# DeltaNet attention with a folded feed-forward on one core: odd heads on the other partition half, weight signs on GpSimd, second inverse in PSUM, a new order of work

## The chip, the core and the metric

The kernel runs on one core of one Trainium2 chip. The metric is the time of one execution on the device in microseconds (us). The kernel before takes 628.66 us, the median of 3 runs (627.59 to 628.71). A profile is one more execution, recorded by the hardware profiler. Its *span* is a little shorter than the time, because the time also holds the start and the end: the profiled execution of before had a span of 623.6 us and a time of 625.4 us. The runs of a program on one core can fall into a slower state.

Engine names in the profile: PE is the matrix engine, PEld its weight loads (they overlap PE), DVE the vector engine, ACT the scalar engine, POOL is GpSimd, SP the engine that issues most DMA transfers. L474 is line 474 of the kernel that was profiled, so the same statement has different numbers in different kernels.

## The reference

The attention is a delta rule with one 48 x 48 state for each of 4 batches and 8 heads, over 768 steps. The feed-forward part takes its result as 3072 tokens of 384 features.

```python
# q, k, v: (B=4, H=8, S=768, D=48), beta: (B, H, S)
k_n = k / (norm(k) + 1e-6)
for t in range(S):
    y[:, :, t] = q[:, :, t] @ state
    v_old = state^T k_n[:, :, t]
    state = state + beta_t * outer(k_n[:, :, t], v[:, :, t] - v_old)
x = y as (B*S, H*D)                    # 3072 x 384
a, b = x @ w1, x @ w2                  # 384 x 1024 each
out = ((a * b) @ w3) @ w_out           # 1024 x 1024, 1024 x 384; weights come as float64
```

## The kernel before

The sequence is cut into 12 chunks of 64 tokens. Inside a chunk the delta rule becomes the inverse of a triangular 64 x 64 matrix for each head and batch, some products with it, and an update of the state. Two chunks make a pair, and each pair feeds 512 tokens to the feed-forward part. There the product w3 @ w_out is formed once (`fold`), so that only three large products remain per token: with w1, with w2 and with the folded weight.

The program is a set of generators (`scores`, `inverse`, `chain`, `ab`, `piece` and so on). A long string, ORDER, names the generator that takes its next step. Every engine executes its instructions in exactly that order. Its letters: `P` weight pieces, `V` inverses, `c` chain, `s` scores, `g` and `N` sums of squares and norms, `a` and `o` feed-forward products, `f` folding.

The weights arrive as float64 and are converted with integer arithmetic, in 36 pieces. For each piece ACT scales twice, DVE shifts and puts the sign in, and GpSimd adds the low bits exactly:

```python
def piece(n, srcs, dst):
    raw = in_turn(ffn, [P, CW, 2], "raw", 5, "raw", U32)      # five raw buffers
    ...                                                       # DMA on the SP queue
    act.activation(out=dst, in_=hi.bitcast(FP32), func=ACTF.Abs, scale=2.0**-112)
    act.activation(out=lo, in_=lo, func=ACTF.Copy, scale=2.0**-29)
    yield
    dve.tensor_scalar(out=du, in0=du, scalar1=3, scalar2=None, op0=ALU.logical_shift_left)
    dve.scalar_tensor_tensor(
        out=du, in0=hi, scalar=0x80000000, in1=du, op0=ALU.bitwise_and, op1=ALU.bitwise_or
    )
    yield
    pool.tensor_tensor(out=du, in0=du, in1=lo, op=ALU.add)
```

The inverse of a pair is 31 steps of two DVE operations. Its working matrix V is in SBUF, except for the first pair, where it is held in PSUM:

```python
    V = Vb                                  # SBUF
    if j == 0:
        V = two_banks().rearrange("p a (s t) -> p (a s) t", t=BS)    # PSUM
        ...
    for s in range(BS - 1):
        ...                                 # tb = V * U
        dve.tensor_tensor(out=o, in0=o, in1=tv, op=ALU.subtract)
        yield
```

The small products of the chain are 64 x 64 or 48 x 64 tiles. I call the half of the 128 partitions on which a product's inputs lie its row half, the half on which its output lies its column half, and the pair of the two a *quarter*; there are four. In `by_tokens`, which makes X, both halves are `half(z)`, so that only the two diagonal quarters are used:

```python
    def by_tokens(ps, r, h, z):
        return ps[half(z), r, D * h : D * h + D]
    ...
    ps = products(
        by_tokens, lambda r, h, z: TT[half(z), r, h, :], lambda r, h, z: R[half(z), r, h, :]
    )
```

## Time and profile before

| | before |
|---|---|
| time, median of 3 | 628.66 us |
| span of the profiled execution | 623.6 us |
| first feed-forward matmul with w1 starts | 139.44 us |
| PE busy after that | 479.2 of 480.4 us |
| PE busy before that | 101.1 of 139.4 us, clock 0.85 |
| first feed-forward product taken by DVE | 155.98 us |

I call what lies before 139.4 us the *front* and what follows the *dense part*. The prediction below shows the lines and reads them in this order.

One more view divides the front of before into three legs along DVE's work: first inverse, from the first to the second inverse, second inverse. The columns are start and end, length, then busy time and instructions of PE, PEld, DVE, ACT and POOL, the granted PE clock, the DMA share and GB/s.

```profile
44.13:74.30 30.17, 23.88 (x74) 14.68 (x73) 27.86 (x78) 11.98 (x25) 12.77 (x12) 0.84 0.85 192
74.30:123.39 49.09, 44.89 (x917) 32.01 (x918) 40.69 (x68) 26.41 (x51) 23.03 (x22) 0.86 0.77 176
123.39:155.90 32.51, 28.21 (x145) 14.44 (x134) 30.41 (x71) 11.41 (x25) 6.50 (x5) 0.95 0.76 128
```

The third column of busy times is DVE: 27.9 of 30.2 us, 40.7 of 49.1, 30.4 of 32.5. DVE is the busiest engine in the first and the last leg. A blocked DVE instruction counts as busy here.

### The profile page before, as it was taken

To read this page: it belongs to the slowest core of one execution; us is meant where nothing else is said; L and a number is where in the kernel's file an instruction comes from. 1 tells how busy PE (TensorE), PEld (TensorE's weight loads), DVE (VectorE), ACT (ScalarE), POOL (GpSimd) and SP (SyncE) were. 2 spreads that over 40 slices of the span, in tenths; PEclk is the share of its full clock that TensorE was granted. 3 is DMA by queue.
4 is the path that set the end of the run, shared out by engine and by line. 5 is a ranking of instruction groups with operands and counts; after the bars stand their busy time and mean duration, and the time that the engine had idled before them with its cause. 6 is when DMAs were issued, how large, how long until landed. Compare 5 with 4: busy or idle time off the path is not lost.

```text
span 623.6 us, 17022 instructions
## 1 busy us (share of the span) xinstructions
PE 580.3 (93%) x7372; PEld 343.1 (55%) x7372; DVE 352.2 (56%) x764; ACT 161.1 (26%) x333; POOL 102.1 (16%) x114
## 2 busy tenths in 40 slices
PE   3838779979999999999999999999999999999997
PEld 2724457744575655665556655466564556545454
DVE  3599879999856674667827659464397032100100
ACT  3573236642241112311113111123011022210100
POOL 5364453402321100201002010120001000000000
PEclk9857888999999999999999999999999999999999
DMA  9678966886742724443444453333311200000001
GB/s 207 163 211 169 239 153 140 195 150 107 174 65 52 126 76 87 64 77 80 70 106 52 68 120 73 68 67 43 69 40 39 72 23 3 26 14 25 0 14 38
DMA packets 201835, 55.60 MB, mean 89 GB/s; under 512 B 191969, under 2 KB 195041, under 8 KB 201761
## 3 DMA queue, kind: packets, MB, share of 16 engines
q1 hardware_dynamic: 197600, 53.74, 41.7%
q10 hardware_dynamic: 4160, 0.79, 0.8%
q8 instruction: 58, 0.95, 0.7%
q14 instruction: 17, 0.13, 0.1%
HBM read 42.30 MB, written 11.01 MB: 85 GB/s over the span
## 4 chain that ended last, share of the span: by engine, by line
PE 81%; DMA 7%; SPq 4%; DVE 3%; issue 2%; ACT 2%; POOL 1%; DVEq 0%; ACTq 0%; POOLq 0%
PE ps_f L694 41%; PE ps_f L714 20%; PE ps_w L474 6%; PE ps_w L569 4%; PE ps_w L322 3%; DMA raw<-in_moe_w_dram 3%; SPq L212 2%; PE ps_t L444 2%; PE ps_t L430 2%; PE ps_f L674 2%; DMA vtok<-in_v_dram 1%; DMA ktok<-in_k_dram 1%; DMA X<-in_q_dram 1%; DMA raw<-in_moe_w_out_dram 1%; SPq L614 1%
## 5 line engine op out<-in xcount | busy, mean ns | idle before, releaser
L694 PE MATMUL ps_f<-xT,w1s 128*128 128x512 f32 x288 | 132.9, 605 | 4.3 <-DMA xT<-xT 4.3
L694 PE MATMUL ps_f<-xT,w2s 128*128 128x512 f32 x288 | 131.7, 599 | 0.0
L714 PE MATMUL ps_f<-w,ab 128*128 128x384 f32 x384 | 126.4, 488 | 0.0
L714 PEld LDWEIGHTS ps_f<-w,ab 128*128 128x128 f32 x384 | 72.5, 190 | 51.1 <-issue 3.0
L708 DVE TENSOR_TENSOR ab<-a,ps_f 128x512 f32<-128x512 f32 x48 | 32.5, 683 | 112.7 <-PE ps_f L694 112.6
L694 PEld LDWEIGHTS ps_f<-xT,w1s 128*128 128x128 f32 x288 | 53.9, 192 | 66.0 <-issue 63.2
L694 PEld LDWEIGHTS ps_f<-xT,w2s 128*128 128x128 f32 x288 | 53.1, 190 | 60.3 <-issue 56.8
L703 ACT COPY a<-ps_f 128x512 f32<-128x512 f32 x48 | 27.5, 586 | 142.6 <-PE ps_f L694 132.9
L391 DVE TENSOR_TENSOR tb<-Vb,Ub 128x31 f32<-128x31 f32 (+15 forms) x155 | 55.5, 358 | 13.0 <-DMA Ub<-Ud 8.2
L396 DVE TENSOR_TENSOR Vb<-Vb,tb 128x31 f32<-128x31 f32 (+15 forms) x155 | 58.4, 377 | 5.3
L674 PE MATMUL ps_f<-w2s,w3T 128*128 128x384 f32 x128 | 50.0, 550 | 3.6 <-POOL w2s L630 2.1
L234 POOL TENSOR_TENSOR sq<-ktok 128x384 f32<-128x384 f32 x24 | 20.7, 862 | 152.0 <-DVE ss L236 91.6
L590 ACT COPY xT<-ps_w 48x256 f32<-48x256 f32 x96 | 30.4, 365 | 54.2 <-PE ps_w L569 53.7
L720 ACT COPY osb<-ps_f 128x384 f32<-128x384 f32 x24 | 11.3, 479 | 127.4 <-PE ps_f L714 109.1
L460 POOL TENSOR_TENSOR vtok<-vtok,n 128x384 f32<-128x384 f32 x24 | 19.9, 842 | 130.6 <-DMA vtok<-in_v_dram 104.3
L674 PEld LDWEIGHTS ps_f<-w2s,w3T 128*128 128x128 f32 x128 | 26.8, 215 | 23.3 <-issue 6.9
L322 PE MATMUL ps_w<-KQ 48*64 48x128 f32 x768 | 30.5, 303 | 5.3 <-DVE KQ L285 2.7
L322 PEld LDWEIGHTS ps_w<-KQ 48*64 48x64 f32 x768 | 25.0, 150 | 13.9 <-issue 5.5
L665 PE MATMUL ps_f<-ident,w 128*128 128x128 f32 x64 | 13.4, 363 | 13.5 <-POOL w L630 13.5
L630 POOL TENSOR_TENSOR w<-w,raw 128x512 uint32<-128x512 uint32 x16 | 21.2, 1332 | 26.6 <-ACT w L622 7.8
L534 DVE TENSOR_TENSOR S<-S,ps_w 48x768 f32<-48x768 f32 x20 | 19.0, 949 | 11.0 <-PE ps_w L474 10.7
L331 DVE TENSOR_TENSOR U<-ps_w,wt 128x512 f32<-128x512 f32 x24 | 16.4, 686 | 15.0 <-PE ps_w L322 14.6
(83 smaller groups left out, 558.3 us busy)
## 6 DMA issues: line engine op xcount, KB each, us to landing
raw<-in_moe_w_dram SPq DMA_DIRECT2D x16, 512.0 KB, 6.2
vtok<-in_v_dram SPq DMA_DIRECT2D x24, 192.0 KB, 4.0
raw<-in_moe_w_dram SPq DMA_DIRECT2D x24, 192.0 KB, 4.0
out_dram<-osb SPq DMA_DIRECT2D x24, 192.0 KB, 2.0
ktok<-in_k_dram SPq DMA_DIRECT2D x22, 192.0 KB, 4.3
raw<-in_moe_w_out_dram SPq DMA_DIRECT2D x8, 384.0 KB, 3.8
Ud<-U SPq DMA_DIRECT2D x48, 64.0 KB, 2.0
Ub<-Ud SPq DMA_DIRECT2D x6, 512.0 KB, 4.6
```

Of the source, the lines that this page charges most:

```text
L322: pe.matmul(ps[half(z), h % 2, 128 * (h // 2) : 128 * (h // 2) + 128], lhsT=x[:, 0, :], rhs=x.rearrange("p j t -> p (j t)"), start=True, s ...
L391: dve.tensor_tensor(out=tv, in0=V[:, 0 : s + 1, s : s + 1].to_broadcast([P, s + 1, n]), in1=U[:, s, s + 1 : BS].unsqueeze(1).to_broadcast( ...
L396: dve.tensor_tensor(out=o, in0=o, in1=tv, op=ALU.subtract)
L474: pe.matmul(out(ps, r, h, z), lhsT=lhs(r, h, z), rhs=rhs(r, h, z), start=True, stop=True,)
L569: i = pe.matmul(region(h, z, r), lhsT=lhs, rhs=rhs, start=part[n] not in part[:n], stop=part[n] not in part[n + 1 :],)
L590: act.copy(out=xT[f, p:NP:2, b : b + NR, cc, :].rearrange("p a r t -> p r a t"), in_=pyv[f, z, b : b + NR],)
L630: pool.tensor_tensor(out=du, in0=du, in1=lo, op=ALU.add)
L674: pe.matmul(ps[:, 0:DM], lhsT=w3Ts[jc, kc // 4][:, kc % 4 * P : kc % 4 * P + P], rhs=wo[:, kc], start=(kc == 0), stop=(kc == KF - 1),)
L694: pe.matmul(ps[:], lhsT=w[:, m, js], rhs=x[:, m].rearrange("p b c t -> p (b c t)"), start=(m == 0), stop=(m == KM - 1),)
L703: act.copy(out=a[:], in_=ps[:])
L708: dve.tensor_tensor(out=t[:], in0=a[:], in1=ps[:], op=ALU.mult)
L714: pe.matmul(ps[:, 0:DM], lhsT=abs_[u, jc][:, b * P : (b + 1) * P], rhs=w34[:, jc, :], start=(jc == 0), stop=(jc == KF - 1),)
```

## The change

It is four things in one diff.

1. *Crossing.* The keys, the masked scores and X of the odd heads move to the other partition half. The product that makes X and the product that uses it then rotate over all four quarters of the array. It costs twice the DMA issues for k (four of 96 KB for a chunk instead of two of 192 KB), scores of odd heads as two matmuls of 64 columns instead of one of 128, and an exchange (`across`) of the norms' sums and of the weights between the halves, twice for each pair.
2. *Signs.* DVE's sign operation goes. ACT takes the sign of the high word, GpSimd multiplies by it.
3. *Second inverse in PSUM* (`if j < 2`).
4. *A new ORDER*, different from the first step to the last, made for the new operations.

```diff
 ORDER = """
-P3 P6 k0 g0 q0 P3 P3 P3 g0 g0 k1 K0 K0 P6 P6 K0 K0 K0 Q0 Q0 Q0 Q0 Q0 g0 g0 g0 g0 K1 K1 K1 K1
+P6 k0 q0 K0 g0 k1 beta K0 K0 K0 P0 P6 K0 g0 P11 g0 Q0 g0 Q0 g0 g0 g0 P6 P6 g0 q1 Q0 Q0 Q0 P0
 ... (all other lines of the string differ too)
+    def across(src, dst):
+        ...
+        for z in range(2):
+            pe.matmul(
+                psv[half(1 - z)], lhsT=ident[half(z), half(z)], rhs=odd[half(z), 1],
+                start=True, stop=True,
+            )
+        yield
+        dve.tensor_copy(out=even[:, 0], in_=odd[:, 0])
+        dve.tensor_copy(out=even[:, 1], in_=psv)
 ... scores:
-                    pe.matmul(
-                        ps[half(z), h % 2, 128 * (h // 2) : 128 * (h // 2) + 128],
-                        lhsT=x[:, 0, :], rhs=x.rearrange("p j t -> p (j t)"),
+                    if h % 2 == 0:
+                        (as before)
+                    else:
+                        for j in range(2):
+                            pe.matmul(
+                                ps[half(z ^ j), 1, n + C * j : n + C * j + C],
+                                lhsT=x[:, 0, :], rhs=x[:, j, :], start=True, stop=True,
+                            )
 ... inverse:
-        if j == 0:
+        if j < 2:
 ... chain:
-        def by_tokens(ps, r, h, z):
-            return ps[half(z), r, D * h : D * h + D]
+        def crossed(ps, r, h, z):
+            g = NP * r + h // 2
+            return ps[half((z + h) % 2), h % 2, D * g : D * g + D]
 ... outputs:
-                        todo.append((h, z, r, X[half(z), r, h, :], PT[half(z), r, h, :]))
+                            x = half((z + h) % 2)
+                            todo.append((h, z, r, X[x, r, h, :], PT[x, r, h, :]))
 ... piece:
+        act.activation(out=hi.bitcast(FP32), in_=hi.bitcast(FP32), func=ACTF.Sign)
         yield
         dve.tensor_scalar(out=du, in0=du, scalar1=3, scalar2=None, op0=ALU.logical_shift_left)
-        dve.scalar_tensor_tensor(
-            out=du, in0=hi, scalar=0x80000000, in1=du, op0=ALU.bitwise_and, op1=ALU.bitwise_or
-        )
         yield
         pool.tensor_tensor(out=du, in0=du, in1=lo, op=ALU.add)
+        pool.tensor_tensor(out=dst, in0=dst, in1=hi.bitcast(FP32), op=ALU.mult)
```

## The prediction

> **What bounds the kernel now.** I began with the busy shares and slices of the page, cut the span where the first feed-forward matmul starts, and asked for the busy times of both stretches.
>
> ```profile
> PE   3838779979999999999999999999999999999997
> DVE  3599879999856674667827659464397032100100
> POOL 5364453402321100201002010120001000000000
> PEclk9857888999999999999999999999999999999999
> 0.00:139.40 139.40, 101.11 (x1484) 71.37 (x1484) 109.12 (x227) 68.61 (x132) 60.99 (x65) 0.85 0.82 181
> 139.40:619.80 480.40, 479.18 (x5888) 271.72 (x5888) 243.06 (x538) 92.02 (x202) 41.07 (x49) 1.00 0.32 62
> ```
>
> The last two rows give length, then busy PE, weight loads, DVE, ACT, POOL, the granted clock, DMA share and GB/s. There are two kernels here. After 139.4 us PE is busy for 479.2 of 480.4 us at full clock: whatever shortens a PE instruction shortens the run, and other engines cost nothing unless they starve PE. Before it, PE is busy for 101 of 139 us at clock 0.85. DVE is busy for 109 and DMA for 82%; there a chain through DVE, the DMA queue and PE decides when the dense part begins. So time = start of the dense part + its PE work + about 4 us of last store.
>
> What releases the dense part I read from the timeline and the chain of waits:
>
> ```profile
> 139.44 1.19 PE L694 MATMUL ps_f<-xT,w1s 128*128 128x512 f32 x1 [4.30 <-DMA xT<-xT]
> 155.98 0.68 DVE L708 TENSOR_TENSOR ab<-a,ps_f 128x512 f32<-128x512 f32 x1
> ```
>
> PE waited only 4.3 us for xT, but DVE could first take a feed-forward product at 155.98, right after the second inverse (123.39 to 155.9) ended in its order. Three result banks and four a-halves bridge those 16.5 us and hardly more. The end of the second inverse is therefore the second gate, and an earlier xT alone would gain little.
>
> Why DVE is slow there is visible when GpSimd works beside it:
>
> ```profile
> 63.33 1.28 POOL L630 TENSOR_TENSOR w<-w,raw 128x512 uint32<-128x512 uint32 x1 [1.27 <-DVE w L626]
> 63.44 0.43 DVE L396 TENSOR_TENSOR ps_w<-ps_w,tb 128x255 f32<-128x255 f32 x1
> ...
> 127.20 1.28 POOL L630 TENSOR_TENSOR w1s<-w1s,raw 128x512 uint32<-128x512 uint32 x1 [2.55 <-DVE w1s L626]
> 127.29 1.33 DVE L396 TENSOR_TENSOR Vb<-Vb,tb 128x112 f32<-128x112 f32 x1
> ```
>
> In PSUM (first inverse) 255 columns take 0.43 us beside GpSimd; in SBUF (second inverse) 112 columns take 1.33 us, until GpSimd is done. Undisturbed they take 0.28.
>
> **The Trainium skill.** (1) "SBUF — State Buffer", section "SBUF: two separate sides": DVE and GpSimd share one port pair as an exclusive lock, taken by a DVE instruction with two SBUF inputs or in a 2-port mode. The four lines agree. (2) "VectorE: DVE Perf Modes", "The perf-mode tier table": fp32 tensor_scalar from SBUF runs 2x, tensor_tensor 1x. The trace agrees (TENSOR_SCALAR of 512 columns undisturbed 0.42 us, the two-input sign operation 0.69), so the remaining TENSOR_SCALAR can be blocked by GpSimd too; one took 1.32. (3) "TensorE: Matmul & The Clock Gate", "LDWEIGHTS": columns / 1.2 ns, so 64 columns are 53 ns. Next paragraph. (4) Same page, Part 3: tiles of different position run together.
>
> **Part 1, inverse products on four quarters.** Same 64 weight columns, same 48 moving columns:
>
> ```profile
> L474 PE MATMUL ps_w<-R,TT 64*64 64x48 f32 x704 | 22.7, 219 | 0.0
> L474 PE MATMUL ps_w<-S,KQ 48*64 48x48 f32 x704 | 12.6, 220 | 0.0
> L322 PE MATMUL ps_w<-KQ 48*64 48x128 f32 x768 | 30.5, 303 | 5.3 <-DVE KQ L285 2.7 <-ACT KQ L307 2.4 <-ACT xT L590 0.2
> ```
>
> R,TT sits on the two diagonal quarters and costs 22.7/704 = 32.2 ns each; S,KQ uses all four and costs 12.6/704 = 17.9. Two of 32.2 are 64 ns, four of 17.9 are 72: both near the load of one quarter (53 ns by the skill, plus gaps), so each quarter is limited by its weights and two more quarters nearly double the rate. The change makes R,TT (with the first chunk's vtok,TT) rotate over four quarters. I count 640 of the 768 instructions after the first feed-forward matmul: 640 x 14.3 ns = -9.2 us; 128 in the front, where PE has slack.
>
> **Part 2, scores.** Odd heads split a 128-column matmul into two of 64, because the masked part must land on the other half: per chunk 96 PE instructions instead of 64. Moving columns are unchanged; only loads are added. A warm chunk takes 1.91 us (chain of waits), 16 rounds of about 119 ns on four quarters. An odd quarter now needs two rounds like S,KQ, 2 x 58 to 67 ns = 117 to 134. I take +7%, 0.13 us a chunk, 8 chunks in the dense part: +1.0 us. If the new order hinders overlap it could be +30%, +4.6 us.
>
> **Part 3, crossing of norms and weights.** Twelve times two tiny matmuls through a feed-forward bank and two DVE copies. PE pays mainly the switch: a lone block of six feed-forward matmuls takes 2.77 us against 2.58 inside a run, 0.19; with the matmuls I put 0.25 each, eight in the dense part: +2.0. DVE: 24 copies, by the 0.2 us of its small operations 5 us in all, hidden.
>
> Dense part: -9.2 + 1.0 + 2.0 = -6.2 us.
>
> **Part 4, signs on GpSimd.** Removed from DVE: 36 sign operations, 15.5 + 11.1 + 5.6 = 32.2 us, nearly all in the front. Added to ACT: 36 Sign, like the 36 scalings there (23.2 us): 68.6 + 23 is harmless in some 120. Added to GpSimd: 36 multiplies like its adds, 21.2 + 15.7 + 8.3 = 45.2 us, about 30 of them (38 us) before the dense part: 61 + 38 = 99 of 120 us. That is close.
>
> **Part 5, second inverse in PSUM; new order.** I summed undisturbed durations in DVE's order. To the end of the second inverse: 117 us before (actual 155.9, the rest is waiting), 96 after. By legs: the first inverse, 44.13 to 74.3, starts about 2 us earlier (no blocked sign operations ahead; its data could come at 39.5) and loses 4.3 us of signs, of which about 1.3 comes back in blocked TENSOR_SCALARs: -5. From there to the second inverse DVE falls from 36 to 27 us of work. The DMA queue between the store of the first inverse (75.4) and the load of the second's U (118.8) goes from 52 issues in 43.4 us to 43; in proportion -7.5. DVE and queue agree: -8. The second inverse, 32.5 us, loses 2.8 us of signs and some 3 of blocking, takes 1.7 us more TENSOR_SCALAR work: -4. Sum -17. GpSimd at above 80% will block TENSOR_SCALARs and hold raw buffers longer, so the queue stalls: +4. Front: -13; dense part from about 126.
>
> DMA allows it: the front moved 181 GB/s x 139.4 us = 25 MB. The new order issues two fewer w1/w2 pieces (1 MB) and one chunk fewer of small kperm transfers before xT, and can raise its 82% share a little. It would not allow -25.
>
> Total: 628.7 - 13 - 6.2 = 609.5, say 609 us.
>
> **Rivals.** (a) GpSimd becomes the bound in the front: its last adds and the raw buffers hold back weights and with them the folding on PE. For: 99 of 120 us and slow two-input work (1.33 us per 512 columns). Against: the piece rate is also set by DMA (512 KB, 6.2 us to landing), and GpSimd is idle in long stretches now. Front gain 3: 619. (b) The dense part starves: it comes earlier, while DVE still owes the third inverse and GpSimd weight pieces; the inverse held in PSUM leaves one two-bank buffer for chain and scores. For: DVE's sevens to nines up to slice 30. Against: DVE loses work overall and the first inverse already lived so. Some +5: 614. (c) Scores and crossings cost more than I put, up to +8 on PE, eating part 1: 615. (d) The front follows DVE's relief of 21 us fully: 601. (e) Nothing gained in front, part 1 cancelled: 628, needs (a) and (c) together.
>
> **Range and chances.** The front is the wide term, -3 to -21; the dense part -9 to 0. Together 80% within 598 to 621. Two per cent is 616.1: I give 0.76 to faster, 0.22 to same, 0.02 to slower.
>
> **What would show it.** R,TT near 18 ns each, 13.7 us in all; scores at 2.0 to 2.1 us a warm chunk; crossings at 0.25; first w1s matmul at 120 to 130, second inverse ending about 15 us later without 1.3 us steps; PE in the stretch after it above 99% busy and 474 us long. Wrong if the first w1s matmul comes after 135 with GpSimd busy before it, or if idle PE appears behind it, or if the scores' instructions rise above 2.5 us a chunk.

## The result, and the profile after

The changed kernel takes 611.0 us, the median of 4 runs (610.54 to 613.09), against 628.22 us for the kernel before in 4 runs (627.59 to 628.71). The ratio is 0.9733 with a 95% interval from 0.9707 to 0.9759: faster. The output is correct. A ratio in this document is the mean time of one kernel's fast runs over that of the other's of the same rounds, so it is not quite the ratio of the medians that are quoted.

The profiled spans are 623.6 and 608.8 us, a difference of 14.8 us. The medians differ by 17.2 us, because the profiled run of before was a quick one (625.4 us against its median of 628.2). What follows explains the 14.8.

These are the slices of the page of after, in tenths of busy time.

```profile
PE   3728998989999999999999999999999999999997
DVE  2659975578745954766964539675384231101100
POOL 5778866576340010200031001310000000000000
PEclk9856997999999999999999999999999999999999
```

In the first ten slices GpSimd's row now has fives to eights, where before it had nothing above six and mostly three to five. PE's row has eights and nines from the fourth slice on. The same execution in two stretches, cut where its first w1 matmul starts:

```profile
0.00:130.70 130.70, 98.17 (x1629) 69.27 (x1629) 88.06 (x206) 84.55 (x161) 92.69 (x93) 0.86 0.79 182
130.70:605.00 474.30, 470.67 (x6176) 263.99 (x6176) 235.70 (x547) 98.33 (x211) 52.31 (x58) 1.00 0.34 67
```

The front is 130.7 instead of 139.4 us long, so 8.7 us came from there. In it DVE fell from 109.1 to 88.1 us of work, and GpSimd rose from 61.0 to 92.7. The dense part is 474.3 instead of 480.4 us long, so it gave 6.1 us. PE's work there fell by 8.5 us (479.18 to 470.67), but its gaps grew from 1.2 to 3.6 us.

The two gates in the timeline of after, the first w1 matmul and the first product that DVE could take, are these:

```profile
130.69 1.53 PE L742 MATMUL ps_f<-xT,w1s 128*128 128x512 f32 x3 [1.60 <-DMA xT<-xT]
...
147.32 0.68 DVE L756 TENSOR_TENSOR ab<-a,ps_f 128x512 f32<-128x512 f32 x1
```

Both moved by the same 8.7 us (139.44 to 130.69, 155.98 to 147.32). The distance between them is 16.5 and 16.6 us. The end of the second inverse is again the second gate; here DVE does two more operations between (and waits 0.67 us for keys), so the product comes 1.6 us after it instead of 0.1.

In the groups of after, the columns are engine, operation, output and inputs, shapes and count, then busy time in us and the mean in ns of one. A mean is from start to modelled end, and such small matmuls overlap: the rate is busy time over count.

```profile
L517 PE MATMUL ps_w<-R,TT 64*64 64x48 f32 x704 | 12.9, 220 | 0.1
L618 PE MATMUL ps_w<-PT,X 64*48 64x64 f32 x768 | 12.9, 216 | 0.0
L251 PE MATMUL ps_f<-wt,ident 64*64 64x16 f32 x24 | 1.8, 220 | 0.0
L251 PE MATMUL ps_f<-ss,ident 64*64 64x16 f32 x24 | 1.8, 219 | 0.7 <-ACT w L729 0.6
```

R,TT took 22.7 us and takes 12.9, which is 12.9 / 704 = 18.3 ns each against 32.2. The product of masked scores and X also became cheaper. In the groups of before it read:

```profile
L569 PE MATMUL ps_w<-PT,X 64*48 64x64 f32 x768 | 16.1, 219 | 0.1
```

That is 3.2 us less for the whole run, which I had not predicted. Its even heads and its odd heads used to run in two separate modes; now all rotate over four quarters in one. The versions below show that both savings are the crossing's: R,TT takes 22.7 to 23.1 us and masked scores by X 16.1 to 16.4 us in every kernel without it, 12.6 to 14.5 and 12.9 to 13.5 in every one with it, whatever the order. That a quarter is limited by its weights, as the prediction says, and not by something else that the quarters do not share, no run tests.

The same three legs of the front in after:

```profile
41.85:70.86 29.01, 23.18 (x68) 13.54 (x69) 27.15 (x70) 19.36 (x36) 24.94 (x22) 0.75 0.85 224
70.86:110.92 40.06, 36.45 (x784) 26.46 (x783) 27.49 (x54) 26.59 (x51) 27.00 (x24) 0.91 0.72 157
110.92:145.72 34.80, 32.72 (x337) 17.94 (x336) 25.45 (x74) 20.96 (x41) 24.10 (x21) 1.00 0.79 168
```

The first leg starts 2.3 us earlier and is 1.2 us shorter. The middle leg is 9.0 us shorter. The third leg has 5.0 us less of DVE work (30.41 to 25.45) and yet is 2.3 us longer: DVE's idle time in it rose from 2.1 to 9.35 us. What it waits for stands in the timeline of after:

```profile
115.02 0.67 ACT L671 ACTIVATE w1s<-raw 128x512 f32<-128x512 f32 x1 [1.80 <-DMA raw<-in_moe_w_dram]
115.72 0.43 DVE L675 TENSOR_SCALAR w1s<-w1s 128x512 uint32<-128x512 uint32 x1 [3.54 <-ACT w1s L671]
...
135.53 0.68 ACT L671 ACTIVATE w2s<-raw 128x512 f32<-128x512 f32 x1 [5.44 <-DMA raw<-in_moe_w_dram]
136.24 0.43 DVE L675 TENSOR_SCALAR w2s<-w2s 128x512 uint32<-128x512 uint32 x1 [2.69 <-ACT w2s L671]
```

The order places the shifts of weight pieces between steps of the inverse. Here the inverse stands still because a piece is not there: DVE waits for ACT, and ACT waits for the DMA of the raw weights. Four such gaps (3.54, 2.69, 0.88 and 0.41) make 7.5 us. The queue shows why. These are the issues of weight pieces on the SP queue during the second inverse of before (start, how long the issues took, and their number; a piece of w1 or w2 is four issues):

```profile
125.96 3.67 SPq L614 DMA_DIRECT2D raw<-in_moe_w_dram  x8
...
131.09 3.56 SPq L614 DMA_DIRECT2D raw<-in_moe_w_dram  x4
...
145.85 1.72 SPq L614 DMA_DIRECT2D raw<-in_moe_w_dram  x4
```

And of after:

```profile
107.88 8.35 SPq L663 DMA_DIRECT2D raw<-in_moe_w_dram  x12
...
117.76 5.29 SPq L663 DMA_DIRECT2D raw<-in_moe_w_dram  x8
...
130.56 1.92 SPq L663 DMA_DIRECT2D raw<-in_moe_w_dram  x4
...
135.39 4.20 SPq L663 DMA_DIRECT2D raw<-in_moe_w_dram  x8
```

The new order brings eight pieces (32 issues) through the queue in this leg, the old one four (16 issues). From 107.4 to 145.7 us the queue of after is issuing for 37.4 of 38.3 us. It is full, and the inverse waits for what stands in it. How much of a piece's lateness is its issue and how much its transfer is not separated here: the DMA engines were busy for 79% of this leg, in before for 76%.

### The profile page after: what moved, and what is told of

Read it like the earlier page. It is cut to its first block, busy times and chain, and to the rows that moved or that the text cites.

```text
span 608.8 us, 17988 instructions
## 1 busy us (share of the span) xinstructions
PE 569.2 (94%) x7804; PEld 333.2 (55%) x7804; DVE 323.8 (53%) x752; ACT 183.4 (30%) x373; POOL 145.0 (24%) x150
## 4 chain that ended last, share of the span: by engine, by line
PE 71%; DMA 8%; SPq 8%; DVE 6%; POOL 2%; issue 2%; ACT 1%; POOLq 0%; DVEq 0%; ACTq 0%
PE ps_f L742 36%; PE ps_f L762 21%; SPq L226 4%; PE ps_w L517 4%; PE ps_w L618 3%; DMA raw<-in_moe_w_dram 2%; PE ps_t L487 2%; SPq L663 2%; PE ps_w L366 2%; PE ps_t L473 1%; PE ps_w L360 1%; DVE ps_w L439 1%; DVE tb L434 1%; DMA Ub<-Ud 1%; DVE w L675 1%
## 5 line engine op out<-in xcount | busy, mean ns | idle before, releaser
L742 PE MATMUL ps_f<-xT,w1s 128*128 128x512 f32 x288 | 131.1, 598 | 1.6 <-DMA xT<-xT 1.6
L762 PE MATMUL ps_f<-w,ab 128*128 128x384 f32 x384 | 127.3, 488 | 0.0
L266 POOL TENSOR_TENSOR sq<-ktok 128x384 f32<-128x384 f32 x24 | 20.6, 858 | 156.5 <-DVE ss L268 98.9
L434 DVE TENSOR_TENSOR tb<-Vb,Ub 128x31 f32<-128x31 f32 (+15 forms) x124 | 43.5, 351 | 7.1 <-DMA Ub<-Ud 3.1
L439 DVE TENSOR_TENSOR Vb<-Vb,tb 128x31 f32<-128x31 f32 (+15 forms) x124 | 43.0, 347 | 4.3
L768 ACT COPY osb<-ps_f 128x384 f32<-128x384 f32 x24 | 11.4, 479 | 109.6 <-PE ps_f L762 81.5
L360 PEld LDWEIGHTS ps_w<-KQ 48*64 48x64 f32 x384 | 25.8, 152 | 9.7 <-ACT KQ L343 4.0
L366 PE MATMUL ps_w<-KQ 48*64 48x64 f32 x768 | 30.9, 241 | 0.0
L581 DVE TENSOR_TENSOR S<-S,ps_w 48x768 f32<-48x768 f32 x20 | 19.0, 949 | 19.3 <-PE ps_w L517 14.4
L366 PEld LDWEIGHTS ps_w<-KQ 48*64 48x64 f32 x768 | 28.5, 153 | 0.1
L713 PE MATMUL ps_f<-ident,w 128*128 128x128 f32 x64 | 11.4, 320 | 14.4 <-POOL w L678 12.1
```

The source lines that it names most:

```text
L360: pe.matmul(ps[half(z), 0, n : n + 128], lhsT=x[:, 0, :], rhs=x.rearrange("p j t -> p (j t)"), start=True, stop=True,)
L366: pe.matmul(ps[half(z ^ j), 1, n + C * j : n + C * j + C], lhsT=x[:, 0, :], rhs=x[:, j, :], start=True, stop=True,)
L434: dve.tensor_tensor(out=tv, in0=V[:, 0 : s + 1, s : s + 1].to_broadcast([P, s + 1, n]), in1=U[:, s, s + 1 : BS].unsqueeze(1).to_broadcast( ...
L742: pe.matmul(ps[:], lhsT=w[:, m, js], rhs=x[:, m].rearrange("p b c t -> p (b c t)"), start=(m == 0), stop=(m == KM - 1),)
L762: pe.matmul(ps[:, 0:DM], lhsT=abs_[u, jc][:, b * P : (b + 1) * P], rhs=w34[:, jc, :], start=(jc == 0), stop=(jc == KF - 1),)
```

## The experiments

The prediction added up parts. So the first theory was: **the parts act separately**, each is worth what its own operations save, and the order only has to fit. The first rival was that **the new order itself** brings the front's gain, whatever the operations. The second was that **the parts are worth something only in an order made for them**. A further rival, (a) of the prediction, was that **GpSimd bounds the front** now. Twelve kernels were run, in three jobs on the chip, all with a correct result. One timed run of b_all and three of a_nocross were slow; medians and ratios leave them out. Medians of before in the three jobs: 628.61, 628.15 and 628.0 us. The changed kernel was not run again in these jobs; "slower than after" compares with its 611.0 us, which holds to about the 0.6 us by which the medians of before differ. "Before" and "after" name the operations and the order that a version starts from.

| version | order | operations | median us | minus before of its job | ratio, 95% interval |
|---|---|---|---|---|---|
| b_sign | old | before + signs | 638.66 | +10.0 | 1.0153 (1.0116 to 1.0191) |
| b_v1 | old | before + PSUM inverse | 627.69 | -0.9 | 0.9990 (0.9956 to 1.0023) |
| b_cross | old | before + crossing | 665.78 | +37.2 | 1.0606 (1.0569 to 1.0642) |
| b_all | old | all of after | 672.37 | +43.8 | 1.0700 (1.0638 to 1.0762) |
| b_order | new | before | 642.75 | +14.6 | 1.0222 (1.0174 to 1.0270) |
| a_nosign | new | after, signs undone | 616.08 | -12.1 | 0.9798 (0.9754 to 0.9841) |
| a_nov1 | new | after, PSUM inverse undone | 623.14 | -5.0 | 0.9911 (0.9884 to 0.9938) |
| a_nocross | new | after, crossing undone | 632.06 | +3.9 | 1.0039 (1.0014 to 1.0065) |
| b_cross2 | old, exchanges later | before + crossing | 651.9 | +23.9 | 1.0390 (1.0353 to 1.0428) |
| a_exch | new, exchanges earlier | after | 624.98 | -3.0 | 0.9949 (0.9931 to 0.9967) |
| a_actq | new | after, 16 loads on ACT's queue | 624.98 | -3.0 | 0.9958 (0.9937 to 0.9979) |
| a_half | new | after, 8 of 36 signs back | 612.65 | -15.4 | 0.9763 (0.9722 to 0.9804) |

### b_sign: the signs alone, in the old order

```diff
+        act.activation(out=hi.bitcast(FP32), in_=hi.bitcast(FP32), func=ACTF.Sign)
-        dve.scalar_tensor_tensor(out=du, in0=hi, scalar=0x80000000, in1=du, ...)
+        pool.tensor_tensor(out=dst, in0=dst, in1=hi.bitcast(FP32), op=ALU.mult)
```

> The kernel before, its own order, with the signs alone moved from DVE to ACT and GpSimd. Theory (the front is a chain in which DVE, the DMA queue and the order share): DVE loses some 28 us of busy time, but the queue's order is as before, so the first w1s matmul moves from 139.4 to about 135 and the time falls by 4 us (1 to 8). Rival 1 (the signs alone make the front's gain): first w1s at about 130, -9 us. Rival 2 (GpSimd becomes the bound without the new order): no gain or slower, with GpSimd above 85% busy before the first w1s matmul.

It is 10 us slower instead of faster. The dense part begins at 148.93 us, 9.5 us later than in before, so the loss is in the front. The longest wait of PE in b_sign (total, times, longest) is:

```profile
PE ps_f L662 <- POOL w L627: 25.6, 6, 8.5
```

In before the same wait, of the transposes of w3 for GpSimd's result, was 13.5 us. Here GpSimd is busy for 94.9 us of the front, about as in after (92.7). That is 64% of the longer front, not the 85% that rival 2 named. What differs is when the result is asked for: the old order places the transposes for the old GpSimd work, and each piece now takes GpSimd twice as long. This is read from the waits (after, with the same work in its own order, waits for 12.1 us there); no run moved the transposes alone.

### b_v1: the second inverse in PSUM alone, in the old order

```diff
-        if j == 0:
+        if j < 2:
 (twice; and four more V1 steps in the order, for the copies into and out of PSUM)
```

> The kernel before, its own order, with the second inverse alone in PSUM. Theory: the blocked steps of the second inverse (some five of over 1 us) vanish, it ends 3 to 4 us earlier less 1.2 us of copies; xT comes as before, so the time falls by 0 to 3 us. Rival (the held two-bank buffer starves chain and scores): slower by 2 us or more, with PE waiting for ps_w.

The time did not move clear of noise (ratio 0.999, interval across 1), which lies in the range. The inverse did get shorter, from 32.5 to about 29 us, but it started 4 us later (127.3 instead of 123.4), and the dense part began at 144.43. The first product that DVE took came at 157.58, against 155.98. The later start need not be the edit's: DVE was 3.5 us behind before's trace at 101 us already, ahead of every step of the second inverse, and the profiled run was the slowest of the four (629.08). The old order has few GpSimd operations beside this inverse (6.5 us of POOL in before's third leg), so there was less blocking to escape than in the new one.

### b_cross and b_all: the crossing alone, and all three parts, in the old order

The first builds of this version deadlocked and were not run: with a fixed order, an exchange can wait for a bank that only a later step frees. So in b_cross the exchange uses the bank of `corner`, and one step of `corner` moved up a little in three of the six pairs:

```diff
-        ps = bank([P, n, NR, NP])
+        ps = in_turn(psT, [P, n, NR, NP], "t", 1, "ps_t")
 (otherwise the code of after, with `if j == 0` and the sign operation of before;
  the 24 steps of the exchanges stand directly behind the sums and the norms)
```

> The kernel before, its order, with the crossing alone (crossed loads, scores, products, outputs and the 12 exchanges, which here take the corner's PSUM bank instead of a feed-forward bank so that the old order stays free of deadlock). Theory: the dense part is 6 us shorter, the front unchanged: -6 us (4 to 9), R,TT at 18 ns each. Rival (exchanges and scores eat it when the order was not made for them): within 2 us of before.

b_all is the code of after in the old order, with the same bank for the exchange and the same placing.

> All three parts of the change in the old order (exchanges in the corner's PSUM bank). Theory: -6 from the crossing and about -5 from the front, -11 us, so the new order is worth some 6 us by itself on top. Rival (the new order is worth nothing by itself): -17 us, as the change.

Both missed by far: +37 us and +44 us. PE's longest waits in b_cross:

```profile
PE ps_t L249 <- DVE wt L297: 18.0, 5, 4.2
PE ps_f L712 <- POOL w L677: 16.2, 4, 5.4
```

The exchange is a matmul whose input is the end of a chain of 15 small DVE operations. Standing directly behind it in the order, it makes PE wait for that chain, 18.0 / 5 = 3.6 us on average. The work itself was predicted at 0.25 us, and measured in after at (1.8 + 1.8) / 12 = 0.3. Here the price of an exchange is the wait, not the work. The waits are not the only loss. The dense part of b_cross begins at 154.3 and is 506.7 us long with PE busy for 486.65, at a clock of 0.96; after needs 470.67 us for as many instructions at a clock of 1.00. So the 8.5 us that the crossing saves on PE in after do not appear here. Why the clock is lower was not tested.

The parts add up among themselves: +10.0 - 0.9 + 37.2 = +46.3 against +43.8 for all three together, whose fast runs lie between 668 and 676 us. So the sum shows no interaction beyond the noise. The order is what turns a loss of 44 us into a gain of 17. (b_all differs from after in the exchange's bank too, so this compares the order with that bank. And "the old order" includes my placing of the exchanges: b_cross2 below takes 13.9 us of the loss away by another one.)

### b_order: the new order with the operations of before

The code of before, with the string of after less the 28 steps that only the new operations have.

> The new order alone, with the kernel before's operations. Theory: the order was made for a relieved DVE; alone it gives the queue's part of the front, -3 us (-7 to +3) against before. Rival (the order makes the front's gain): -9 us or more.

It is 14.6 us slower, where I expected a gain of 3. The first rival falls: the order has no gain of its own. Its stretches:

```profile
134.40:637.10 502.70, 485.00 (x5889) 273.19 (x5887) 250.52 (x551) 94.69 (x204) 44.27 (x51) 0.99 0.32 63
```

The dense part starts 5 us earlier than in before, but it holds 17.7 us of idle PE. The second inverse runs from 115.83 to 159.65, 43.8 us, and DVE takes the first product only at 161.47, 27 us after the dense part began. The distance that is bridged without loss was 16.5 us. About half of the idle time, 9.0 us, falls between 142 and 164 us, around this late product; most of the rest, 7.7 us, comes later, has no releaser in the profile and is looked at under a_nocross.

### a_nosign: after, with the signs back on DVE

The three edits of b_sign, reversed, in the code of after.

> The changed kernel with its order, the signs put back on DVE alone. Theory: DVE regains 30 us before the dense part, first w1s matmul from 130.7 to about 137, time some 6 us above the changed kernel (617). Rival (the front's gain is the new order of the DMA queue): within 2 us of the changed kernel (611).

It came as expected, 5 us slower than after. The first w1 matmul is at 135.07 and the first product at 153.56. DVE is busy for 101.5 us of that front, against 88.1 in after. In the new order the signs are worth 5 us on GpSimd; in the old one they cost 10.

The second inverse of this version is telling. It has the same weight pieces beside it, and DVE does their signs as well; yet it takes 35.4 us (115.52 to 150.97), only 0.6 more than in after. DVE's waits for pieces in it are 1.83 and 0.18 us instead of 7.5:

```profile
119.34 0.43 DVE L672 TENSOR_SCALAR w1s<-w1s 128x512 uint32<-128x512 uint32 x1 [1.83 <-ACT w1s L669]
...
140.76 0.43 DVE L672 TENSOR_SCALAR w2s<-w2s 128x512 uint32<-128x512 uint32 x1 [0.18 <-ACT w2s L669]
```

So in this leg the relief from the signs seems to have been spent almost wholly on waiting for the same pieces.

### a_nov1: after, with the second inverse back in SBUF

```diff
-        if j < 2:
+        if j == 0:
 (twice; four V1 steps out)
```

> The changed kernel with its order, the second inverse back in SBUF alone. Theory: GpSimd is 70% busy beside it, so many of the 62 steps wait for it (up to 1 us each); the inverse takes some 6 to 10 us more and the dense part starves by about as much: 616 to 620 us. Rival (the inverse was not on the path): 611.

It is 12 us slower than after, more than I expected. The second inverse takes 44.9 us (114.11 to 159.01) instead of 34.8. One pair of steps shows it. In a_nov1, with V in SBUF:

```profile
134.28 1.39 DVE L437 TENSOR_TENSOR Vb<-Vb,tb 128x255 f32<-128x255 f32 x1
```

In after, with V in PSUM, at the same shape:

```profile
128.02 0.43 DVE L439 TENSOR_TENSOR ps_w<-ps_w,tb 128x255 f32<-128x255 f32 x1
```

GpSimd works beside this inverse in both, for 24.8 us in a_nov1 and 24.1 in after. DVE's busy time in it, which holds the time in which an instruction is blocked, is 40.8 us in a_nov1 and 25.5 in after. The new order puts many weight pieces beside this inverse. That is worth it only with the inverse in PSUM; b_order shows what the same order does without.

### a_nocross: after, without the crossing

The keys, scores, X and outputs as before; the 24 steps of the exchanges taken out of the new order.

> The changed kernel's order with signs on GpSimd and the second inverse in PSUM, but without the crossing. Theory: the dense part is 6 us longer, plus 1 us: about 617 to 618. Rival (the crossing's worth is hidden in the order): 611.

It is 21 us slower than after, where I expected 6 to 7. The front is as good as in after (first w1 matmul 129.78, first product 147.04). Its dense part:

```profile
129.80:622.70 492.90, 479.79 (x5889) 271.42 (x5888) 235.76 (x534) 99.29 (x214) 53.37 (x59) 1.00 0.33 64
```

PE is busy for 9.1 us more than in after (479.79 against 470.67), which is the crossing's own worth on PE: it agrees with the 8.5 us between before and after. The other 9.5 us are idle time (13.1 against 3.6). Most of that idle time, 8.4 us in six stretches, the profile lays to no releaser. The 20 runs spread from 625.0 to 636.3 us, and the profile fell in one of the quicker ones (628.21), so the two halves explain its span and not the whole 21 us.

The trace has more to say of the 8.4 us. b_order, which shares the order and lacks the crossing too, has six such stretches at nearly the same places of PE's stream, 7.7 us; before and after have none of over 0.5 us. The pages list a queue q8 "instruction" that moves 16 KB at a time: 58 transfers in kernels with 7372 matmul records and as many weight loads, 61 in those with 7804. All six stretches of a_nocross end 1.3 to 1.5 us after such a transfer has ended, as do those of b_order. In all twelve versions together there are 35 of over 0.5 us, and each ends 1.3 to 1.8 us after one. So PE most likely waited for its own next instructions. Why they come late with this order and without the crossing was not tested.

This version also answers another question. It loads k in two transfers per chunk, as before does, and yet DVE waits for the same two weight pieces inside the second inverse for 3.14 and 2.88 us. So the extra k issues of the crossing are not what makes the pieces late.

### b_cross2: the old order with the exchanges later

If the wait for the weights' exchange is what makes b_cross slow, it should shrink when the exchange stands just before the product that needs it.

```diff
-N0 N0 N0 P15 s0 s0 s0 q1 ... s1 f0 e1 c0
+N0 P15 s0 s0 s0 q1 ... s1 f0 e1 N0 N0 c0
 (likewise for the other five pairs)
```

> As the crossing alone in the old order, but the six exchanges of the weights stand later in PE's order, just ahead of the product whose result they scale, instead of directly behind the norms. Theory (PE executes in order and stood still for 18.0 us before these exchanges while DVE worked out the norms): the time falls from 665.8 by about 20 us, to 640 to 650, and the wait for DVE wt is gone from PE's list. Rival (the crossed loads or the scores cost it): it stays above 660.

The wait of 18.0 us is gone, and the time fell by 13.9 us, from 665.78 to 651.9, just short of the expected 640 to 650. That settles the largest single part. The remaining 24 us above before have many small parts. In the profiled run the front is 10.6 us longer than in before (150.0), and PE is idle for 17.4 us in the dense part instead of 1.2. The largest wait of PE that is left is

```profile
PE ps_f L712 <- POOL w L677: 15.7, 4, 4.9
```

It is near the 13.5 us of before. What causes the rest was not resolved.

### a_exch: after, with the exchanges earlier

The same test from the other side. The second half of `norms` is moved directly behind the first in the new order (for the third pair nine steps behind).

```diff
-... beta P7 N0 P7 P7 s0 s0 s0 ... t3 N0 P4 P1 P13 P2 P2 V0 t3 P10 P10 t2 P13 N0
+... beta P7 N0 N0 N0 P7 P7 s0 s0 s0 ... t3 P4 P1 P13 P2 P2 V0 t3 P10 P10 t2 P13
```

> The changed kernel with one thing of its order undone: the exchanges of the weights stand directly behind the norms in program order. Theory: PE waits some 3 to 4 us at each of five exchanges in the dense part and front, +10 to +18 us: 621 to 629. Rival (with this order DVE is done early and the place does not matter): within 3 us of 611.

It is 14 us slower than after, within the range, and the wait is back:

```profile
PE ps_f L249 <- DVE wt L297: 14.7, 5, 5.7
```

No operation was added or removed here. Twelve steps in another place cost 14 of the 17 us that the change brings.

### a_actq: after, with 16 query loads on ACT's queue

The SP queue is full in the front. So I tried to relieve it of the 16 small query loads of chunks 2 and 3.

```diff
-                        sync.dma_start(
+                        dma = act.dma_start if m < 4 and src is q else sync.dma_start
+                        dma(
```

> The changed kernel with the 16 query loads of the third and fourth chunk issued from ACT's queue instead of SP's. Theory (between 79 and 107 us the front is a chain of back-to-back issues on SP's queue): first w1s matmul from 130.7 to about 127, time -2 to -4 us. Rival (PE's folding and the weights behind GpSimd set it): within 2 us, or slower where ACT stands still for a buffer.

It is 14 us slower than after, where I expected 2 to 4 us less. Chunk 3's loads show why. In after they were issued on the SP queue between 89.4 and 95.0 us. In a_actq:

```profile
95.39 0.59 ACT L495 ACTIVATE TT<-ps_t 32x512 f32<-32x512 f32 x1 [0.85 <-PE ps_t L488]
...
100.82 0.86 ACTq L227 DMA_DIRECT2D qperm<-in_q_dram  x2
```

ACT issues in its own order, so the loads stand behind its copies and scalings, and come 11 us later. PE then waits 11.1 us for the transposed queries (it waited 0.5 in after), the second inverse starts at 124.36 instead of 110.92, and the dense part at 143.34 instead of 130.69. The load is on the path of the front, but moving it to a busy engine makes it late.

### a_half: after, with 8 of the 36 signs back on DVE

If GpSimd bounded the front, taking 8 of its 36 multiplies away should help. If DVE did, giving it 8 sign operations should hurt.

```diff
-        act.activation(out=hi.bitcast(FP32), in_=hi.bitcast(FP32), func=ACTF.Sign)
+        if not dve_sign:
+            act.activation(out=hi.bitcast(FP32), in_=hi.bitcast(FP32), func=ACTF.Sign)
 (and the sign operation of before `if dve_sign`; set for every second piece of w3)
```

> The changed kernel with the signs of 8 of the 36 pieces (every other w3 piece) back on DVE. If GpSimd is the bound of the front, 10 us less work there bring the first w1s matmul 3 us or more forward (608 or below). If DVE is, +1 to +2 us (a quarter of the 5 us that all signs cost). Theory: both are balanced by the order, within 2 us of 611.

Within 2 us of after, as expected (612.65 against 611.0). GpSimd's front work fell by 11 us (92.7 to 81.5) and DVE's rose by 4 (88.1 to 92.0), and the first w1 matmul moved by half a microsecond, to 130.18. Inside the second inverse DVE still waits for the piece of w2:

```profile
136.18 0.43 DVE L676 TENSOR_SCALAR w2s<-w2s 128x512 uint32<-128x512 uint32 x1 [1.80 <-ACT w2s L671]
```

The waits for pieces in this leg are 2.73, 1.80, 1.16, 0.49 and 0.42 us, 6.6 in all, against 7.5. 11 us off GpSimd and 4 us onto DVE moved the front by less than a microsecond, so GpSimd alone does not bound it, unless what one engine gained the other lost: the test moves both at once.

No version beat the changed kernel. a_actq and a_half were the two that might have.

## Why the prediction was right, point by point

The prediction was 609.0 us, the result 611.0 us, inside the range, and faster by more than 2% as given the best chance.

**Dense part: right, with luck in the last digit.** Predicted -6.2 us, measured -6.1. By terms: the product on four quarters was put at 640 x 14.3 ns = -9.2 us and gave -8.8 in the dense part (20.6 to 11.8 us), because its rate came to 18.3 ns and not 17.9. The exchanges were put at +2.0 and cost 1.1 + 1.1 = 2.2. The split scores were put at +1.0, a chunk at 2.0 to 2.1 us. Their two groups overlap in time; merged, they are busy for 17.2 us in the dense part against 16.5, so +0.7, and an undivided chunk takes 2.10 us against 1.98. Two terms were missing, and that they cancel is luck: masked scores by X took 2.6 us less in the dense part (13.4 to 10.8), and 2.4 us of new gaps in PE opened. The second is rival (b) in a small size.

**Front: right in kind, too large.** Predicted -13 us, measured -8.7. By legs:

| leg | predicted | measured |
|---|---|---|
| first inverse, with its start | -5 | -3.4 (74.3 to 70.9) |
| from there to the second inverse | -8 | -9.0 (49.1 to 40.1) |
| second inverse | -4 | +2.3 (32.5 to 34.8) |
| allowance for GpSimd and a stalling queue | +4 | inside the legs |
| sum | -13 | -10.1 at the end of the second inverse, -8.7 at the first product |

Three sizes were off. In the first leg the signs took 6.2 us (4.3 are those of w2s alone), but the seven shifts left there rose from 2.9 to 7.0 us, so blocking by GpSimd gave back 4.1 us and not 1.3; the leg itself became 1.2 us shorter instead of 3. And the signs before the dense part were 26.3 of the 32.2 us, so not nearly all.

The step that failed is "The second inverse, 32.5 us, loses 2.8 us of signs and some 3 of blocking, takes 1.7 us more TENSOR_SCALAR work: -4". As a count of DVE's work it was right: 5.0 us less was measured. But 1.7 us more of shifts means four more weight pieces in this leg, and they must have arrived. I counted what DVE does with them and not when they come. They come through a queue that issues without a pause, and DVE stands idle 7.3 us longer. The allowance of +4 named the queue as a risk, and was too small for it. I had laid the stall to GpSimd holding raw buffers. That cause is not what the runs show. In this leg the queue itself waited for only 2.6 us, none of it for GpSimd. a_nocross, with two k loads for a chunk instead of four, kept the two large waits. And a_nosign fits a pace that the pieces set: with DVE slower by their signs, the leg took 0.6 us longer and the waits were nearly gone. What is left as the likely cause of the late pieces is their number in a queue that issues without a pause, with the transfer time itself as a rival. I did not run a version with fewer pieces in this leg, so that last step is read from the queue and not shown by an experiment.

**What I had named to look for.** The product near 18 ns (18.3), a PE above 99% busy in a dense part of 474 us (470.67 / 474.3 = 99.2%, 474.3 us), an inverse that ends 15 us after the first w1 matmul (145.7 - 130.7) and has no steps of 1.3 us: all there. The first w1 matmul, named for 120 to 130 us, came just outside, at 130.69.

**Signs: sizes right.** DVE's front fell by 21 us (109.1 to 88.1). GpSimd's multiplies were put at 45.2 us and took 45.0. GpSimd was put at 99 us before the dense part and had 92.7. The shifts, which GpSimd can block, rose from 19.3 to 23.5 us over the run.

**Rivals.** (a), GpSimd as the bound, does not fit the changed kernel: a_half moved the front by 0.5 us, and in a_nosign GpSimd works for 57.8 us in the front instead of 92.7 and the dense part begins 4.4 us later. In the old order something like it happened: in b_sign PE's wait for GpSimd rose from 13.5 to 25.6 us. (c), costlier scores and exchanges, did not happen on PE. (d), the full 21 us of DVE's relief, did not come, for the reason above.

**What I did not see at all** is in the table of versions. I took each part for a saving of its own and asked of the order only that it should not spoil it. The runs refute that reading and the second one, that the order does it. From before, each single part is worth nothing or costs: -0.9, +10.0, +37.2, and the order alone +14.6. From after, undoing any one loses: 5 us for the signs, 12 for the inverse, 21 for the crossing, and 14 for twelve misplaced steps. With the exchanges placed as in b_all, the order is worth 43.8 + 17.2 = 61.0 us with the new operations, and -14.6 us with the old ones. So "the dense part is PE's work only" holds for both kernels only because each has an order in which every input is ready in time.

What stays open: why PE's instructions come late in a_nocross and b_order (if they are the cause of the idle time there), why the clock is lower in b_cross, and the last 24 us of b_cross2.

## What to carry to other kernels

Where engines execute in a fixed order, price a new operation by when its input is ready at its place and not only by its duration: here an exchange of 0.3 us made PE wait 3 to 4 us when it stood directly behind the chain that feeds it. When a change hands an engine more pieces to process in a stretch, check that the queue can bring them there as well. And a part of a change that loses in the old order may still be worth having: judge it together with an order made for it, by undoing it from the final version.

## What the Trainium skill lacked or had wrong

- "TensorE: Matmul & The Clock Gate", Part 3, "What overlaps and what doesn't", says that a weight load overlaps running matmuls only when its row group differs. Here R,TT already alternated between the two row halves and ran at 32.2 ns each; with the second column half added to each row half it runs at 18.3 ns. By that sentence alone the column half should make no difference. The speed-ups for packing by columns in the same part, "Measured speedup vs the span model", fit the runs better, so it is the sentence that is too narrow.
- "DMA: Bandwidth & Descriptors", "Issuing engines are not separate DMA queues", says that issuing from several engines saves only the sequencer's time, which is usually small beside the transfer. Here the issues filled the queue: SP was issuing for 37.4 of 38.3 us around the second inverse, and DVE idled 9.35 us there. That another engine's queue would have helped is not shown; the one try, a_actq, lost. The page also does not say that a transfer on a compute engine's queue waits in that engine's order: the loads moved to ACT were issued 11 us later, and the kernel lost 14 us.
- No page has it: how far a wait in the order of one engine reaches. Twelve steps in another place, with no operation added, cost 14 us (611.0 to 624.98).
